# DeltaNet with routed experts: whole triangular inverses on VectorE, compact states, smaller tiles for Q times state and logits

## The chip, the cores and the metric

One core of one Trainium2 chip. The metric is the device time of one execution in microseconds (us), the median of several runs.

## The reference

Four batches, eight heads, 768 tokens, head dimension 48. A delta-rule attention runs token by token, and its output goes through a top-1 mixture of eight experts (3072 tokens, 384 -> 1024 -> 384):

```python
k_n = k / (norm(k) + 1e-06)
for t in range(S):
    y[:, :, t] = q_t @ state
    state = state + b_t * outer(k_t, v_t - k_t @ state)
x = y as (3072, 384)
logits = x @ w_gate; e = argmax; gate = softmax(logits)[e]
out = gate * (relu(x @ w1[e]) @ w2[e])
```

## The kernel before

**Blocks and steps.** The tokens are cut into 24 blocks of C = 32; a block holds all four batches (32 partitions each) and eight heads (four pairs p, and e = 0, 1 inside a pair). `step(c)` carries the state from block to block: K times state into `pc` (L366), R = V - K state on VectorE (L372), `pz` = inverse times R (L390), Z by ScalarE (L397), two half updates of `acc` in PSUM with copies of it into `states` behind each (L406, L417, L419), and the output `pq` = Q times state (L381) plus masked Q K times Z (L425). `states` holds 96 columns, two heads side by side with zeros between, so that Q times state uses all 128 rows at once.

**Scores.** `scores(c)` makes K K and Q K products of a block (L184); `keep_scores` masks them on VectorE into `gt` and `qk` (L203). In the loop, the block LEAD = 9 ahead of the step is scored; nine are scored ahead of the loop.

**Inverse.** Four blocks make a group g of 32 columns per partition (GS * H). `invert(g)`, a generator, transposes `gt` into `ut` (L222), takes norms by Newton steps, and inverts the two 16x16 triangles on the diagonal together: for each j a product (L281) and an addition (L286). `across(g, s)` fills the corner between them with two small products per block on PE (L316, L330), a ScalarE copy between and a VectorE addition behind (L335).

**Order.** The order is written out by hand. `fill(us)` advances the generators in `behind` until their rated costs (the numbers after `yield`) reach the amount; `chore(n)` runs n of the queued pieces of PE work. `chores` holds crossings, logits and ranks; `behind` holds inverses and routing. Engines run their own instructions in this order. One PSUM tile (`psA`) serves scores and crossings in turn; `psR` serves transposes, logits (L449) and ranks (L494, L497).

**Routing.** Batches of up to four blocks: logits, arg-max, ranks by a matmul with a triangular matrix, then a scatter of row numbers into `lists` by GpSimd (L533), one block each. The rows go to `xs` in DRAM.

**Experts.** Behind the attention, weights of experts 1 and 2 (L109, L110) take the memory that it used; then the lists are read, rows gathered, and eight experts computed in turn (L651 to L698). Expert 0's weights are loaded during step 12.

Of the kernel before, what the change touches and what calls it, by code (L numbers as in the profile page):

```python
# [13 lines left out]
FP32 = mybir.dt.float32  # L14
# [16 lines left out]
E = 8  # L31
# [9 lines left out]
LEAD = 9  # L41
# [4 lines left out]
def _f32_consts():  # L46

    p = np.arange(128)[:, None]
    j = np.arange(128)[None, :]
    rev = np.broadcast_to(E - np.arange(E), (128, E))
    base = np.broadcast_to(np.arange(E) * LIST, (128, E))
    more = np.arange(E)[:, None] * LIST + CAP + np.arange(MAXR)[None, :] * 128
    more = np.broadcast_to(more.reshape(1, -1), (128, E * MAXR))
    t, w = p % C, j[:, :C]
    own = t // (C // 2) == w // (C // 2)
    kk = 1.0 * (t == w) - ((t < w) & own) - (t // (C // 2) > w // (C // 2))
    return np.concatenate(  # L60
        [rev, base, more, p < j, np.ones((128, 128)), kk, t < w], axis=1
    ).astype(np.float32)
# [3 lines left out]
def kernel(  # L66
# [25 lines left out]
    def part(w):  # L92
# [4 lines left out]
    rev, base, further, upper, ones, mask_g, mask_q = (  # L97
        part(w) for w in (E, E, E * MAXR, 128, 128, C, C)
# [26 lines left out]
    psR = att.enter_context(tc.tile_pool(name="psR", bufs=1, space=PSUM))  # L125
# [5 lines left out]
    states = persist.tile([128, 2, 2 * NP, 2 * D], FP32, name="states")  # L131
# [4 lines left out]
    fdts = [persist.tile([128, GS * H, C], FP32, name=f"fdt{i}") for i in range(2)]  # L136

    kqs, kts, vts, qks, gts, ubs, norms, vss = {}, {}, {}, {}, {}, {}, {}, {}
    routed = []
    behind, chores = deque(), deque()  # L140

    def rows_of(b):
        return slice(C * b, C * b + C)

# [4 lines left out]
    def fill(us):  # L149
        while us > 0 and behind:  # L150
            cost = next(behind[0], None)
            if cost is None:
                behind.popleft()
            else:
                us -= cost
# [18 lines left out]
    def scores(c):  # L174
# [5 lines left out]
        for p in range(NP):  # L180
            for b in range(B):
                for e in range(2):
                    r = slice(64 * e, 64 * e + 64)
                    nc.tensor.matmul(  # L184
                        pa[rows_of(b), e, 64 * p : 64 * p + 64],
                        lhsT=kq[r, p, 0, rows_of(b)], rhs=kq[r, p, :, rows_of(b)],
# [4 lines left out]
    def keep_scores(c, pa):  # L191
# [7 lines left out]
        for out, part, mask in (  # L199
            (gts[g][:, H * s : H * s + H, :], view[:, :, :, 0:C], mask_g),  # L200
# [9 lines left out]
    def invert(g):  # L210


        gt = gts[g]
        W = C // 2
        ut = block.tile([128, C * C + C], FP32, name="ut")
        full = ut[:, 0 : C * C].rearrange("p (i j) -> p i j", j=C)
        diag = ut[:, 0 : C * C].rearrange("p (i j) -> p i j", j=C)
        ud = ut[:].rearrange("p (k n) -> p k n", k=2)[:, :, 0 : W * C].rearrange(
            "p k (i j) -> p k i j", j=C
        )  # L220
        ones_at = ut[:, 0 : C * C : C + 1]
        nc.vector.transpose(  # L222
            out=full.rearrange("p i j -> p j i"), in_=gt[:].rearrange("p s j -> p j s")
        )
        yield 1.15

        def short(name, bufs=None):
            return small.tile([128, C], FP32, name=name, **({"bufs": bufs} if bufs else {}))
# [3 lines left out]
        nc.vector.memset(full[:, W:C, 0:W], 0.0)  # L232
        yield 0.3
# [5 lines left out]
        yield 0.2  # L239
        r = seed[:].bitcast(FP32)  # L240
        for _ in range(3):
            t = short("nt", 3)
# [3 lines left out]
            yield 0.2  # L246
            nc.vector.tensor_tensor(out=t[:], in0=t[:], in1=r, op=OP.mult)
            yield 0.2
            rn = short("nr", 3)
# [3 lines left out]
            yield 0.2  # L253
# [3 lines left out]
        yield 0.2  # L257
        nc.vector.tensor_scalar(out=norm[:], in0=norm[:], scalar1=1e-6, scalar2=None, op0=OP.add)
        yield 0.2
        inv = short("inv")  # L260
        nc.vector.reciprocal(out=inv[:], in_=norm[:])
        yield 0.35
        norms[g] = small.tile([128, GS * H], FP32, name="normt", bufs=3)
        nc.vector.transpose(out=norms[g][:], in_=norm[:])
        wt = short("wt")
        nc.vector.tensor_tensor(out=wt[:], in0=inv[:], in1=inv[:], op=OP.mult)
        yield 0.3
        nc.vector.tensor_tensor(out=wt[:], in0=wt[:], in1=beta[:, g, :], op=OP.mult)
        yield 0.2
        w2 = wt[:].rearrange("p (k i) -> p k i", k=2)  # L270
        square = ud[:, :, :, 0:W]
        nc.vector.tensor_tensor(
            out=square, in0=square, in1=w2.unsqueeze(3).to_broadcast([128, 2, W, W]), op=OP.mult
        )
        nc.vector.memset(ones_at, 1.0)
        yield 0.75
        for j in range(W - 2, 0, -1):
            n = W - 1 - j
            tmp = block.tile([128, W * W // 2], FP32, name="tmp", bufs=3)
            tv = tmp[:, 0 : 2 * j * n].rearrange("p (k i w) -> p k i w", k=2, w=n)  # L280
            nc.vector.tensor_tensor(  # L281
                out=tv, in0=ud[:, :, 0:j, j].unsqueeze(3).to_broadcast([128, 2, j, n]),
                in1=ud[:, :, j, j + 1 : W].unsqueeze(2).to_broadcast([128, 2, j, n]), op=OP.mult,
            )
            yield 0.16 + 0.0021 * j * n
            nc.vector.tensor_tensor(  # L286
                out=ud[:, :, 0:j, j + 1 : W], in0=ud[:, :, 0:j, j + 1 : W], in1=tv, op=OP.add
            )
            yield 0.16 + 0.0021 * j * n
        nc.vector.tensor_tensor(  # L290
            out=square, in0=square, in1=w2.unsqueeze(2).to_broadcast([128, 2, W, W]), op=OP.mult
        )
        yield 0.7
        ub = block.tile([128, GS * H, C], FP32, name="ub", bufs=3)
        nc.vector.transpose(
            out=ub[:].rearrange("p s j -> p j s"), in_=full.rearrange("p i j -> p j i")
        )
        yield 1.15
        fdt = fdts[g % 2]
        nc.vector.transpose(  # L300
            out=fdt[:, :, 0:W].rearrange("p s i -> p i s"), in_=full[:, 0:W, :]
        )
        yield 0.6
        ubs[g] = ub
        for s in range(GS):
            chores.append(partial(across, g, s))

    def across(g, s):

        gt, ub, fdt = gts[g], ubs[g], fdts[g % 2]  # L310
# [43 lines left out]
    def step(c):  # L354
# [3 lines left out]
        pz = pc[:, :, 192:384].rearrange("q e (p w) -> q e p w", p=NP)  # L358
        if c == 0:
            R = vs  # L360
        else:
            for p in range(NP):
                for b in range(B):
                    for e in range(2):
                        r = slice(64 * e, 64 * e + 64)
                        nc.tensor.matmul(  # L366
                            pc[rows_of(b), e, D * p : D * p + D], lhsT=kq[r, p, 0, rows_of(b)],
                            rhs=states[r, b % 2, NP * (b // 2) + p, D * e : D * e + D],
                            start=(p == 0), stop=True, skip_group_check=True,
                        )  # L370
# [4 lines left out]
            )  # L375
        scale_v(c + 1)
        pq = psQ.tile([128, DM], FP32, name="pq")
        if c > 0:
            for p in range(NP):
                for b in range(B):  # L380
                    nc.tensor.matmul(  # L381
                        pq[rows_of(b), 96 * p : 96 * p + 96], lhsT=kq[:, p, 1, rows_of(b)],
                        rhs=states[:, b % 2, NP * (b // 2) + p, :],
                        start=(p == 0), stop=False, skip_group_check=True,
                    )
        chore()
        fill(1.2)
# [10 lines left out]
        keep_scores(c + LEAD, pa)  # L398

        def update(first):  # L400

            for p in range(NP):
                for b in range(B):
                    e = b // 2 if first else 1 - b // 2
                    at = D * (NP * (b // 2) + p)
                    nc.tensor.matmul(  # L406
                        acc[64 * e : 64 * e + D, b % 2, at : at + D],
                        lhsT=kt[rows_of(b), 2 * p + e, :], rhs=Z[rows_of(b), 2 * p + e, :],
# [378 lines left out]
```

## Time and profile before

| | before |
|---|---|
| median of three runs | 781.13 us (780.2 to 782.03) |
| profiled execution | 774.58 us, span 772.6 us |
| granted TensorE clock, mean | 0.78 |
| PE matmul busy | 609.1 us (79%), 12596 instructions |
| VectorE busy | 222.5 us (29%), 671 instructions |
| ScalarE busy | 142.6 us (18%), 407 instructions |
| GpSimd busy | 102.0 us (13%) |

PE is TensorE, DVE VectorE, ACT ScalarE, POOL GpSimd. The clock is the share of full speed that TensorE was granted. Busy times are unions over the span; each fp32 matmul appears as two pairs of weight load and matmul, a transpose as one. L numbers are lines of the kernel.

### The profile page before, as it was taken

The numbers are of one execution on the slowest core, as the hardware profiler recorded it, in microseconds if no ns is written. First come the engines' busy times: TensorE is split into PE (matmuls) and PEld (weight loads), VectorE is DVE, ScalarE is ACT, GpSimd is POOL, SyncE is SP. The second block draws the span as 40 slices with busy tenths as digits, with TensorE's granted clock in tenths as the row PEclk, the third lists the DMA queues.
The fourth block names the chain that finished last, engine by engine and source line by source line (L and its number), as shares of the span: only waits on it lengthen the run. The fifth ranks groups of instructions, "written<-read, shape, count | busy, mean of one in ns | idle before, by whom it ended". The sixth has DMA issues, their size and how long they took to land. (4 is left out here: it accounts for less than half of the span.)

```text
span 772.6 us, 27052 instructions
## 1 busy us (share of the span) xinstructions
PE 609.1 (79%) x12596; PEld 419.1 (54%) x12597; DVE 222.5 (29%) x671; ACT 142.6 (18%) x407; POOL 102.0 (13%) x107
## 2 busy tenths in 40 slices
PE   3268886777787578778782089999999999999992
PEld 2257775666676467666672045555555454545450
DVE  3963545155454524611221010101010101010100
ACT  0033221222322123222420000101010101010100
POOL 2000001100200100110103121313131313131010
PEclk9998555555576555555855579999999999999997
DMA  8402103220420620211102810124232423230000
GB/s 299 164 25 74 56 26 118 51 71 26 120 79 25 226 45 25 65 24 45 46 24 65 294 49 21 45 100 121 102 123 102 125 102 124 102 123 20 12 19 11
DMA packets 32339, 63.64 MB, mean 82 GB/s; under 512 B 5942, under 2 KB 23782, under 8 KB 32224
## 3 DMA queue, kind: packets, MB, share of 16 engines
q1 hardware_dynamic: 26640, 51.94, 21.0%
q0 software_dynamic: 4608, 9.47, 4.1%
q8 instruction: 99, 1.62, 0.9%
q10 hardware_dynamic: 976, 0.48, 0.3%
q14 instruction: 16, 0.13, 0.1%
HBM read 53.10 MB, written 10.35 MB: 82 GB/s over the span
## 5 line engine op out<-in xcount | busy, mean ns | idle before, releaser
L660 PE MATMUL phe<-xTe,w1t 128*128 128x448 f32 x384 | 147.6, 545 | 0.0
L676 PE MATMUL pye<-w2t,hT 128*128 128x384 f32 x384 | 125.1, 486 | 0.0
L660 PEld LDWEIGHTS phe<-xTe,w1t 128*128 128x128 f32 x384 | 72.9, 192 | 69.5 <-issue 67.2
L676 PEld LDWEIGHTS pye<-w2t,hT 128*128 128x128 f32 x384 | 73.0, 190 | 51.6 <-issue 3.0
L533 POOL DMA_INDIRECT lists<-ids,ri x24 | 23.5, 978 | 385.9 <-DVE ut L286 142.1
L665 DVE TENSOR_SCALAR hT<-phe 128x448 f32<-128x448 f32 x32 | 20.0, 624 | 126.7 <-PE phe L660 126.7
L640 POOL DMA_INDIRECT out_dram<-y,rows x24 | 24.0, 999 | 210.9 <-ACT y L685 177.5
L406 PE MATMUL acc<-Z,kt 32*48 32x48 f32 x1472 | 41.0, 265 | 13.0 <-issue 6.6
L419 DVE COPY states<-acc 48x384 f32<-48x384 f32 x46 | 25.8, 560 | 88.6 <-ACT states L417 88.5
L184 PE MATMUL pa<-kq 64*32 64x64 f32 x1536 | 29.2, 303 | 27.8 <-issue 18.9
L349 ACT ACTIVATE vs<-vt,normt 128x48 f32<-128x48 f32 x192 | 45.5, 322 | 0.0
L669 ACT ACTIVATE hT<-phe 128x448 f32<-128x448 f32 x32 | 17.4, 543 | 151.6 <-PE phe L660 151.6
L651 PE MATMUL px<-ident,xin 128*128 128x128 f32 (+1 forms) x96 | 18.9, 304 | 32.7 <-issue 30.6
L406 PEld LDWEIGHTS acc<-Z,kt 32*48 32x48 f32 x1472 | 32.6, 170 | 21.0 <-issue 10.4
L425 PE MATMUL pq<-Z,qk 32*32 32x48 f32 x1536 | 34.4, 260 | 9.0 <-issue 8.2
L390 PE MATMUL pc<-R,ub 32*32 32x48 f32 x1472 | 32.5, 260 | 10.6 <-DVE R L372 7.5
L184 PEld LDWEIGHTS pa<-kq 64*32 64x32 f32 x1536 | 22.8, 145 | 31.7 <-issue 20.7
L655 DVE COPY xTe<-px 128x448 f32<-128x448 f32 x24 | 14.1, 612 | 88.6 <-PE px L651 88.6
L316 PE MATMUL po<-ub,gt 32*32 32x16 f32 x1536 | 25.8, 206 | 17.2 <-issue 8.8
L417 ACT ACTIVATE states<-acc 48x384 f32<-48x384 f32 x46 | 22.2, 483 | 88.2 <-PE acc L406 88.2
L330 PE MATMUL po<-m,fdt 32*32 32x16 f32 x1536 | 26.5, 205 | 13.5 <-issue 7.5
L449 PEld LDWEIGHTS pr<-wg,xT 128*128 128x128 f32 x144 | 30.1, 304 | 11.6 <-ACT xT L443 6.9
(96 smaller groups left out, 628.2 us busy)
## 6 DMA issues: line engine op xcount, KB each, us to landing
kq<-in_kq_t_dram SPq DMA_DIRECT2D x24, 512.0 KB, 5.5
w1t<-in_moe_w_dram SPq DMA_DIRECT2D x8, 1536.0 KB, 6.4
w2t<-in_moe_w_dram SPq DMA_DIRECT2D x8, 1536.0 KB, 7.1
kt<-in_k_tok_dram SPq DMA_DIRECT2D x24, 192.0 KB, 3.7
vt<-in_v_tok_dram SPq DMA_DIRECT2D x24, 192.0 KB, 4.0
xs<-xg SPq DMA_DIRECT2D x5, 770.0 KB, 5.0
xs<-xg SPq DMA_DIRECT2D x1, 577.5 KB, 3.8
lists<-ids,ri POOLq DMA_INDIRECT x24, 3.8
```

What stands on the lines that cost most here:

```text
L184: nc.tensor.matmul(pa[rows_of(b), e, 64 * p : 64 * p + 64], lhsT=kq[r, p, 0, rows_of(b)], rhs=kq[r, p, :, rows_of(b)], start=True, stop=Tr ...
L316: nc.tensor.matmul(po[rows_of(b), 0, W * h : W * h + W], lhsT=gt[rows_of(b), sh, :], rhs=ub[rows_of(b), sh, W:C], start=True, stop=True, s ...
L330: nc.tensor.matmul(po[rows_of(b), 0, W * h : W * h + W], lhsT=fdt[rows_of(b), sh, :], rhs=m1[rows_of(b), h, :], start=True, stop=True, ski ...
L349: nc.scalar.activation(out=vss[c][:, h, :], in_=vt[:, h, :], func=AF.Copy, scale=norms[g][:, H * s + h : H * s + h + 1],)
L390: nc.tensor.matmul(pz[rows_of(b), h % 2, h // 2, :], lhsT=ub[rows_of(b), H * s + h, :], rhs=R[rows_of(b), h, :], start=(c == 0 and h < 2), ...
L406: nc.tensor.matmul(acc[64 * e : 64 * e + D, b % 2, at : at + D], lhsT=kt[rows_of(b), 2 * p + e, :], rhs=Z[rows_of(b), 2 * p + e, :], start ...
L419: nc.vector.tensor_copy(out=out, in_=src)
L425: nc.tensor.matmul(pq[rows_of(b), D * h : D * h + D], lhsT=qk[rows_of(b), h, :], rhs=Z[rows_of(b), h, :], start=(c == 0 and h == 0), stop= ...
L449: nc.tensor.matmul(pr[:, DM + E * i : DM + E * i + E], lhsT=xT[:, s, :], rhs=wg[:, s, :], start=(s == 0), stop=(s == NK - 1), skip_group_c ...
L640: nc.gpsimd.indirect_dma_start(out=out, out_offset=bass.IndirectOffsetOnAxis(ap=index, axis=0), in_=y[0:w, :], in_offset=None, bounds_chec ...
L660: nc.tensor.matmul(ph[:], lhsT=w1t[:, s, f * 128 : f * 128 + 128], rhs=xT[:, s, :], start=(s == 0), stop=(s == NK - 1),)
L676: nc.tensor.matmul(py[:], lhsT=hT[:, f, t * 128 : t * 128 + w], rhs=w2t[:, f, :], start=(f == 0), stop=(f == NF - 1),)
```

## The change

The inverse of a group is made whole, 32x32, on VectorE for all groups but the first (K = 1; group 0 keeps K = 2 and the crossing). `ut` is laid out the other way round; its transposes are cut in four pieces each. Rated costs are changed, and `fill` takes turns between the first two generators in `behind`, with a queue `soon` for routing ahead of them. `mask_g` is a full triangle, `mask_0` the old one.

`states` is compact, 48 columns; K and Q blocks are loaded without padding rows, in two transfers of 48 partitions. Q times state uses the same 64-row tiles as K times state. Odd heads' tokens of batch b stand in the partitions of batch b ^ 1 (`rows_at`); V, K and beta are laid out so on the host. The copies of `acc` into `states` are two on ScalarE behind the second update; a small read `seen` stands between the updates. Logits are made in four 32-column parts. Transposes, logits and ranks use the one `psA` tile; `psR` is gone. Eight blocks are scored ahead of the loop (FRONT), then one or two a step until all 24 are scored in step 10. Before each fourth step the inverse of its group is drained.

```diff
-LEAD = 9
+FRONT = 8
+LEAD = 13
...
     def fill(us):
-        while us > 0 and behind:
-            cost = next(behind[0], None)
+        while us > 0 and (soon or behind):
+            from_ = soon or behind
+            cost = next(from_[0], None)
...
+            us -= cost
+            if from_ is behind and len(behind) > 1:
+                behind[0], behind[1] = behind[1], behind[0]
...
-            nc.sync.dma_start(out=kqs[c][:], in_=kq_t[c])
+            for e in range(2):
+                nc.sync.dma_start(out=kqs[c][head(e)], in_=kq_t[c, e])
...
         gt = gts[g]
-        W = C // 2
+        K = 1 if g else 2
+        W = C // K
...
+        for j in range(0, C, 8):
+            nc.vector.transpose(
+                out=full[:, j : j + 8, :], in_=gt[:, :, j : j + 8].rearrange("p s j -> p j s")
+            )
+            yield 0.3
...
+        parts = [(0, W, W)] if K > 1 else [(0, W // 2, W // 2), (W // 2, W, W)]
...
         for j in range(W - 2, 0, -1):
             n = W - 1 - j
...
-            yield 0.16 + 0.0021 * j * n
+            yield 0.09 + 0.00105 * K * j * n
...
+        def by_state(out, i, at):
+            for p in range(NP):
+                for b in range(B):
+                    for e in range(2):
+                        nc.tensor.matmul(
+                            out[at(b, e), e, D * p : D * p + D],
+                            lhsT=kq[head(e), p, i, rows_of(b)],
+                            rhs=states[head(e), b % 2, NP * (b // 2) + p, :],
+                            start=(p == 0), stop=(i == 0), skip_group_check=True,
+                        )
...
+        if turned:
+            logits(*turned.pop())
+        pq = psQ.tile([128, 2, 512], FP32, name="pq")
+        if c > 0:
+            by_state(pq, 1, lambda b, e: rows_of(b))
+        chore()
         scale_v(c + 1)
...
-        fill(1.2)
+        fill(2.6)
...
-        pa = scores(c + LEAD)
+        more = []
+        while scored[0] < min(NS, c + LEAD + 1, FRONT + 1 + c + (c + 1) // 2):
+            for old in more:
+                keep_scores(*old)
+            more = [(scored[0], scores(scored[0]))]
+            scored[0] += 1
...
         if c < NS - 1:
-            update(True)
-        for h in range(H):
+            update(0)
+            seen = small.tile([128, 2], FP32, name="seen")
+            nc.scalar.activation(
+                out=seen[0 : 64 + D], in_=acc[0 : 64 + D, :, 0], func=AF.Copy
+            )
+        for p in range(NP):
+            for b in range(B):
+                for e in range(2):
+                    nc.tensor.matmul(
+                        pq[rows_of(b), e, D * p : D * p + D], lhsT=qk[rows_at(b, e), 2 * p + e, :],
+                        rhs=Z[rows_at(b, e), 2 * p + e, :],
...
+        if c < NS - 1:
+            update(1)
+            for k in range(2):
+                nc.scalar.activation(
+                    out=states[0 : 64 + D, k].rearrange("q s w -> q (s w)"),
+                    in_=acc[0 : 64 + D, k, 0:DM], func=AF.Copy,
+                )
...
+        for s in range(NK):
             for b in range(B):
                 nc.tensor.matmul(
...
+                    pt[rows_of(b), 1, 0:E], lhsT=xT[:, s, rows_of(b)], rhs=wg[:, s, :],
                     start=(s == 0), stop=(s == NK - 1), skip_group_check=True,
                 )
+        nc.scalar.activation(out=lgs[ss[0]][:, c - ss[0], :], in_=pt[:, 1, 0:E], func=AF.Copy)
...
+    for c in range(FRONT):
+        keep_scores(c, scores(c))
+        if c in (GS - 1, GS):
+            fill(4.0)
+        if c == GS + 1:
+            while not ubs:
+                fill(0.1)
+            chore(2)
...
     for c in range(NS):
         load_kq(c + LEAD + 2)
         load_tok(c + 3)
+        if c % GS == 0:
+            while c // GS not in ubs:
+                fill(0.1)
+        step(c)
         chore(2)
+        turn(c)
+        fill(2.0)
+        soon.extend(ranked)
+        ranked.clear()
+        fill(1.8)
```

## Rows read from the trace of the kernel before

**Rows 1.** Busy time by stretches (us, instructions), granted clock, DMA share, GB/s.
```profile
228.00:404.00 176.00, 133.05 (x5115) 113.80 (x5115) 63.53 (x213) 51.07 (x162) 11.67 (x12) 0.59 0.21 58
445.00:772.00 327.00, 310.83 (x992) 165.39 (x990) 42.24 (x72) 35.48 (x64) 68.68 (x68) 0.97 0.23 77
```
**Rows 2.** Timeline of PE in step 17: start, duration, work, count, idle before.
```profile
321.17 1.03 PE L366 MATMUL pc<-states,kq 64*32 64x48 f32 x64
322.13 1.50 PE L381 MATMUL pq<-states,kq 128*32 128x96 f32 x32
323.56 1.45 PE L449 MATMUL pr<-wg,xT 128*128 128x8 f32 x6
325.62 1.50 PE L390 MATMUL pc<-R,ub 32*32 32x48 f32 x64 [0.60 <-DVE R L372]
327.73 0.89 PE L406 MATMUL acc<-Z,kt 32*48 32x48 f32 x32 [0.61 <-ACT Z L397]
328.55 0.86 PE L425 MATMUL pq<-Z,qk 32*32 32x48 f32 x32
...
330.42 0.89 PE L406 MATMUL acc<-Z,kt 32*48 32x48 f32 x32
331.24 1.05 PE L316 MATMUL po<-ub,gt 32*32 32x16 f32 x64
333.64 1.18 PE L330 MATMUL po<-m,fdt 32*32 32x16 f32 x64 [1.36 <-issue]
334.76 0.90 PE L439 MATMUL pr<-ident,xg 128*128 128x128 f32 x3
335.59 0.69 PE L366 MATMUL pc<-states,kq 64*32 64x48 f32 x35
```
**Rows 3.** Timeline: starts of L390 in steps 0, 4, 11 and 23.
```profile
45.65 1.48 PE L390 MATMUL pc<-vs,ub 32*32 32x48 f32 x64
...
108.64 0.88 PE L390 MATMUL pc<-R,ub 32*32 32x48 f32 x64 [0.79 <-DVE R L372]
...
227.96 0.88 PE L390 MATMUL pc<-R,ub 32*32 32x48 f32 x64 [0.25 <-DVE R L372]
...
404.51 1.50 PE L390 MATMUL pc<-R,ub 32*32 32x48 f32 x64
```
**Rows 4.** Timeline of ScalarE: eight V scalings, a copy of states.
```profile
224.78 1.90 ACT L349 ACTIVATE vs<-vt,normt 128x48 f32<-128x48 f32 x8
...
231.62 0.48 ACT L417 ACTIVATE states<-acc 48x384 f32<-48x384 f32 x1 [2.22 <-PE acc L406]
```
**Rows 5.** VectorE groups by line and shape: count, busy us, mean ns, idle before.
```profile
L295 DVE STREAM_TRANSPOSE ub<-ut 128x1024 f32<-128x1024 f32 x6 | 12.2, 2040 | 0.2
...
L290 DVE TENSOR_TENSOR ut<-ut,wt 128x512 f32<-128x512 f32 x6 | 4.2, 692 | 0.2
...
L286 DVE TENSOR_TENSOR ut<-ut,tmp 128x112 f32<-128x112 f32 x12 | 3.3, 274 | 0.4
```
**Rows 6.** Timeline of VectorE: two independent products, then two dependent ones.
```profile
217.13 0.43 DVE L203 TENSOR_TENSOR gt<-pa,cf 128x256 f32<-128x256 f32 x1 [5.59 <-PE pa L184]
217.47 0.41 DVE L203 TENSOR_TENSOR qk<-pa,cf 128x256 f32<-128x256 f32 x1
...
224.38 0.19 DVE L243 SCALAR_TENSOR_TENSOR nt<-ss,seed 128x32 f32<-128x32 f32 x1
224.61 0.19 DVE L247 TENSOR_TENSOR nt<-nt,seed 128x32 f32<-128x32 f32 x1
```
**Rows 7.** Timeline of PE in step 13: the hole in L425.
```profile
269.55 0.70 PE L425 MATMUL pq<-Z,qk 32*32 32x48 f32 x24 [4.34 <-issue]
```
**Rows 8.** Timeline of VectorE: the last transpose of group 0.
```profile
33.76 1.05 DVE L300 STREAM_TRANSPOSE fdt<-ut 128x512 f32<-128x512 f32 x1
```
**Rows 9.** Timeline: last scatter of row numbers, first weight load behind it.
```profile
416.53 0.97 POOL L533 DMA_INDIRECT lists<-ids,ri  x1 [2.95 <-DMA lists<-ids,ri]
...
420.11 0.38 SPq L109 DMA_DIRECT2D w1t<-in_moe_w_dram  x1
```

More of the change, by code (lines that the diff above doesn't have):

```diff
@@ L95, in part @@
         return a
-    rev, base, further, upper, ones, mask_g, mask_q = (
-        part(w) for w in (E, E, E * MAXR, 128, 128, C, C)
+    rev, base, further, upper, ones, mask_g, mask_0, mask_q = (
+        part(w) for w in (E, E, E * MAXR, 128, 128, C, C, C)
     )
@@ L252, in invert @@
             )
-            yield 0.2
+            yield 0.12
             r = rn[:]
@@ L293, in invert @@
-        yield 0.7
-        ub = block.tile([128, GS * H, C], FP32, name="ub", bufs=3)
[L295 to L303, printed above, removed]
+            yield 0.09 + 0.00105 * K * j * n
+        yield from scaled(False)
+        ub = block.tile([128, GS * H, C], FP32, name="ub", bufs=3)
@@ L361, in step @@
         else:
[L362 to L370, printed above, removed]
+            by_state(pc, 0, rows_at)
             R = work.tile([128, H, D], FP32, name="R")
@@ new lines, in step @@
+        for p in range(NP):
[4 more added lines that the diff above has]
+                        rhs=Z[rows_at(b, e), 2 * p + e, :],
+                        start=(c == 0 and p == 0), stop=True, skip_group_check=True,
+                    )
+        ss = first[c]
+        if c == ss[0]:
+            xgs[c] = work.tile([128, GS, ROW], FP32, name="xg")
+            lgs[c] = small.tile([128, GS, E], FP32, name="lg")
@@ new lines, in turn @@
+    def turn(c):
+        ss = first[c]
+        pt = psA.tile([128, 2, 512], FP32, name="pt", tag="pa")
+        for s in range(NK):
+            nc.tensor.transpose(
+                pt[:, 0, 128 * s : 128 * s + 128],
+                xgs[ss[0]][:, c - ss[0], s * 128 : s * 128 + 128], ident[:],
+            )
+        if counted:
+            counted.pop()(pt)
+        xT = work.tile([128, NK, 128], FP32, name="xT")
+        nc.scalar.activation(
+            out=xT[:].rearrange("p s w -> p (s w)"), in_=pt[:, 0, 0:DM], func=AF.Copy
+        )
+        turned.append((c, xT, pt))
@@ L424, in step, with logits @@
+    def logits(c, xT, pt):
+        ss = first[c]
+        for s in range(NK):
             for b in range(B):
                 nc.tensor.matmul(
-                    pq[rows_of(b), D * h : D * h + D], lhsT=qk[rows_of(b), h, :],
-                    rhs=Z[rows_of(b), h, :],
-                    start=(c == 0 and h == 0), stop=True, skip_group_check=True,
-                )
-        fill(0.4)
-        if c < NS - 1:
-            update(False)
-        return pq
-    def logits(xg, i, pr):
-        for s in range(NK):
-            nc.tensor.transpose(
-                pr[:, 128 * s : 128 * s + 128], xg[:, i, s * 128 : s * 128 + 128], ident[:]
-            )
-        xT = work.tile([128, NK, 128], FP32, name="xT")
-        nc.scalar.activation(
-            out=xT[:].rearrange("p s w -> p (s w)"), in_=pr[:, 0:DM], func=AF.Copy
-        )
-        def second():
-            for s in range(NK):
-                nc.tensor.matmul(
-                    pr[:, DM + E * i : DM + E * i + E], lhsT=xT[:, s, :], rhs=wg[:, s, :],
+                    pt[rows_of(b), 1, 0:E], lhsT=xT[:, s, rows_of(b)], rhs=wg[:, s, :],
```

285 lines of the change are left out of this document (132 added, 153 removed).

## The prediction

> **What bounds the kernel now.** I read the table by stretches first [rows 1]. The expert stage (445 to the end) has TensorE (PE) busy for 310.8 of 327 us at a granted clock of 0.97; nothing in the change touches it. [...] The timeline of one step on PE alone [rows 2] shows how a step is spent: 14.42 us from one K times state (L366) to the next, nearly all of it in program order on PE. The first triangular crossing (L316), its copy and the second (L330) take from 331.24 to 334.76, 3.5 us with a 1.36 us "issue" hole in them; Q times state (L381) 1.43, logits (L449) 1.45, Q K times Z (L425) 1.87 to the start of the second update. The rest is the recurrence: L366, R, L390, Z, two updates (L406). So the change must be read as PE time removed per step, and then one must ask whether DVE, which takes over the crossings' work, still fits under what is left.
>
> The steps' marks are the starts of L390, R's product with the inverse [rows 3]: step 0 at 45.65, step 4 at 108.64, step 11 at 227.96, step 23 at 404.51. I forecast these four again, then the tail.
>
> **A late step, no scores (11 to 22).** PE in the new order, at the low clock, start to start from [rows 2]: K times state 0.96; logits; Q times state, now 64 pairs of the shape of L366, 0.96 for 1.43; L390 with the wait for Z 2.11 (325.62 to 327.73); update 0.82; Q K times Z; update 0.82; states. Three terms have no row. Logits become 24 pairs of 128 rows by 32 columns with 8 moving columns. From below: L316's spacing, 64 pairs in 1.05, gives 0.4; from above, not faster than today's 1.45. [...] Q K times Z now alternates between eight tiles of the array, not four: between L366's 0.96, which also has eight, and the 1.43 that four tiles cost in L390; I take 0.96. The states are now two ScalarE copies one after the other; one takes 0.48 [rows 4], so with a start gap of 0.4 and hand-overs of 0.15 each side 1.2, of which the transposes (0.83) cover their own time; DVE's copies go, and with them the wait of the second update, but a small read ("seen") stands there instead, hidden under the 64 pairs of Q K times Z. R (0.55 by interpolation between the 256-element mask product and the 512-element product, [rows 5, 6]) is hidden under logits and Q times state. Sum 8.3. Code loading is extra: a PE idle that ends on "issue" comes back at block boundaries of the instruction stream, and a long one is 4.34 us [rows 7], in the step after the one that asks for expert 0's weights. In this step it shows 1.36 in one piece; I take 1.1 a step, as the step without crossings has 18% fewer pairs of weight load and matmul (347 for 425, by the counts there [rows 2]). A late step is 9.4. From the other side: 14.42 less the crossings 3.5, logits 1.0 and the R wait 0.6, 0.5 for Q times state and 0.7 for Q K times Z is 8.1, plus 0.4 of states that the crossing no longer hides, and a stall of 0.9 that moves elsewhere: 9.4.
>
> **What VectorE must do in it.** Durations by shape [rows 5]: a product of 112 elements 274 ns, of 512 elements 692 ns, so 0.157 + 0.00104 per element; a 1024-element transpose 2.04. A whole 32x32 inverse needs 60 loop instructions on 9920 elements (today 28 on 2240), four scalings (1.1 us a pair), some 22 short ones and eight transposes of 256 elements (about 0.6 each, from 2.04/4 and a fixed part). In busy time that is 19.7 + 2.2 + 4 + 4.5 = 30 us a group; today some 18. But what counts is start to start. The timeline has two independent products that start 0.34 apart though one takes 0.43, and two dependent ones that start 0.23 apart though one takes 0.19 [rows 6]. So an instruction costs its duration less 0.085 beside an independent one, plus 0.035 behind its own input. Two groups in turn: 23 us a group (30 less 0.085 for each of some 90 instructions); one alone: 33. [...]
>
> The order written out gives each step costs of 6.4 (2.6 behind R, 3.8 at its end), and a group is rated 22.5 there, near its 23 interleaved. So DVE needs 0.55 + 6.6 = 7.2 in a late step, under 9.4: hidden. In steps 4 to 10 the mask products add 0.8 a scored token block.
>
> **Steps 4 to 10.** There are ten blocks scored in seven steps. A step with one block: 8.3 less the 0.6 wait for Z, which the scores now cover, plus 1.2 for them (64 pairs of 64 columns, between L366's 1.03 and L390's 1.50 [rows 2]), plus 1.1 of code loading beside K/Q loads: 10.0. With two blocks the second must wait for DVE to read the first out of the one PSUM tile, queued behind 2.6 us of inverse: another 1.2 + 1.0, 12.2. Four and three of them: 76.6. Two batches' routing each stall DVE about 1.5, since the sum over exp waits for ScalarE behind eight V scalings of 1.90 together [rows 4]: 3. Before step 8 the inverse of group 2 is rated some 1.8 short, and draining it in turns costs 3.6. Sum 83.
>
> **Steps 0 to 3.** Here DVE paces. Group 1 must be whole before step 4 and runs alone until block 11 is scored: of its 33 alone some 30 us remain, with 7 for group 2's share, 2 for R, 5 for six blocks' masks, 7 where it stands behind PE for the three crossings of group 0, and some 7 of waits for scores: 58, against 63 now.
>
> **Start.** Group 0 is inverted as today: L300 ends at 34.8 and L390 starts 10.85 later [rows 3, 8]. The crossing now comes ahead of scores 6 and 7, and there are eight blocks, not nine, so the inverse is done one mask pair (0.8) sooner: 34.0, two crossing products with copy and addition 3, scores and masks of two blocks 2 times 2.05, and the next crossing's product with its wait 1.5, together 42.6, three earlier.
>
> **Tail.** The next stage's weights (L109) are issued when the last scatter of row numbers has landed [rows 9], 15.6 after L390 of step 23. The scatters go one at a time: the last waited 2.95 us for the one before it. Now three of batch 5 are issued some 4.5 us later behind that L390, with logits, routing and ranks each one step on, so the fourth lands at about 20.8: 5 us lost. The other DMAs don't matter: 15 K/Q blocks are loaded ahead, in two transfers each of 3/4 of the bytes; one weight load during step 12 keeps its price, 4.
>
> **The sum**, in the profiled execution: 42.6; step 4 at 42.6 + 58 = 101; step 11 at 101 + 83 = 184; step 23 at 184 + 12 times 9.4 + 4 + 3 (draining before step 12) = 304; weights issued at 325 instead of 420.1; and 352.5 from there to the end, unchanged: 677 for 772.6. The execution takes 2.0 more than its span (774.6), and the median of the runs shown, 781.1, is 6.5 above it; 677 + 2 + 6.5 = 686.
>
> **Rivals.** A, VectorE becomes the bound: each of its instructions costs what a dependent one does. For: 60 short instructions a group, in program order ahead of R. Against: 0.34 for 0.43 [rows 6]. Then 6.4 of rated work takes 9.4 (33 for 22.5), a step of 4 to 17 goes to 11.3, 1.3 more on average, and the drains double: 18 + 10, 714. [...] B, the granted clock rises to its upper level as PE's holes go: at that level L390 takes 0.88 for 1.50 [rows 3]. Then a late step is 7.4 and a middle one, held by DVE, a little under 10: 12 times 2.0 + 5, 657. Against: the mean is 0.59 where PE is already busy for 76% [rows 1]. C, code loading takes the gain back: 2.2 a step and not 1.1 in 19 steps with blocks fetched as often per us, 21, and 5 more beside the weight load: 712. D, slower than before: scores, crossings, transposes, logits and ranks now share one PSUM tile, and each hand-over waits for a reader on DVE or ScalarE. If PE stood at it for more than 95/19 = 5.0 us a step beyond the sum, that is behind the whole 3.8 of rated inverse and a second wait, the kernel would be at 783 and above. Against: the order puts the readers ahead of the long fills, the second block's masks excepted. That Q K times Z gains nothing from eight tiles would cost 0.5 times 24, 12 us, and logits at their upper bound 24: inside the range.
>
> **How the numbers follow.** The forecast (670 to 702) 0.56, A 0.18, C 0.12, B 0.11, D 0.03. The range 650 to 735 takes in A, B and C, and, beyond A and C, the bounds of the logits or of the eight tiles for part of the way. A measurement of this kernel can tell about 0.2%; faster by more than that 0.96, within 0.01, slower 0.03.
>
> **What would show it.** Right: L316 and L330 only for group 0; late steps of 9 to 10 us; DVE idle before R in them; starts of two groups' loop instructions closer than one's duration; clock 0.55 to 0.7. A shows as PE waiting for R in most steps; B as L390 of 0.88 throughout; C as "issue" idle of over 40 us; D as PE waiting for masks or lg. I would be most wrong if logits and R don't hide each other, or if the order of DVE's queue blocks R.

## The result and the profile after

The changed kernel took 718.4 us (median) where the kernel before took 781.6 beside it: ratio 0.919 with a 95% interval of 0.913 to 0.924; a second measurement gave 0.919 again (0.915 to 0.924). That is faster, by 63 us where 95 were forecast: inside the range of 650 to 735, well above the forecast of 686. The profiled execution took 713.3, its span is 711.4.

From the page of the changed kernel, first the span, the busy times (share of the span, instructions) and the instruction queue (packets, MB):
```profile
span 711.4 us, 24428 instructions
PE 549.3 (77%) x11204; PEld 359.3 (51%) x11205; DVE 235.4 (33%) x802; ACT 144.1 (20%) x434; POOL 99.9 (14%) x105
q8 instruction: 88, 1.44, 0.9%
```
and the same queue on the page of the kernel before:
```profile
q8 instruction: 99, 1.62, 0.9%
```
TensorE lost 1392 matmuls (12596 before) and as many weight loads, VectorE gained 131 instructions. The queue that brings instructions fell from 99 packets to 88; 1.44 MB in 88 packets is 16.4 KB each, and the 22409 matmuls and weight loads make 255 for each packet.

The four marks, on the timeline of PE: the starts of R's product with the inverse (now L414) in steps 0, 4, 11 and 23; compare [rows 3]:
```profile
43.17 0.82 PE L414 MATMUL pc<-vs,ub 32*32 32x48 f32 x26
...
106.39 0.78 PE L414 MATMUL pc<-R,ub 32*32 32x48 f32 x27
...
203.57 0.70 PE L414 MATMUL pc<-R,ub 32*32 32x48 f32 x24
...
337.17 0.79 PE L414 MATMUL pc<-R,ub 32*32 32x48 f32 x29 [1.25 <-DVE xg L540]
```

| stretch | before | forecast | after |
|---|---|---|---|
| start to step 0 | 45.7 | 42.6 | 43.2 |
| steps 0 to 3 | 63.0 | 58 | 63.2 |
| steps 4 to 10 | 119.3 | 83 | 97.2 |
| steps 11 to 22 | 176.6 | 120 | 133.6 |
| step 23 to the weights' issue | 15.6 | 21 | 22.3 |
| from there to the end | 352.5 | 352.5 | 352.0 |

The two ends came as forecast, the steps between did not. One late step on PE, which answers to [rows 2] (start, duration, work, count, idle before):
```profile
284.60 1.50 PE L414 MATMUL pc<-R,ub 32*32 32x48 f32 x64
286.71 0.89 PE L435 MATMUL acc<-Z,kt 32*48 32x48 f32 x32 [0.61 <-ACT Z L426]
287.53 1.02 PE L451 MATMUL pq<-Z,qk 32*32 32x48 f32 x64
288.48 0.89 PE L435 MATMUL acc<-Z,kt 32*48 32x48 f32 x32
289.30 0.90 PE L479 MATMUL pt<-ident,xg 128*128 128x128 f32 x3
290.13 1.06 PE L388 MATMUL pc<-states,kq 48*32 48x48 f32 x64
291.12 0.38 PE L496 MATMUL pt<-wg,xT 128*32 128x8 f32 x24
291.42 0.69 PE L388 MATMUL pq<-states,kq 48*32 48x48 f32 x50
294.23 0.41 PE L388 MATMUL pq<-states,kq 48*32 48x48 f32 x14 [2.12 <-issue]
294.57 1.50 PE L414 MATMUL pc<-R,ub 32*32 32x48 f32 x64
```
The terms of the sum are there at or below their forecast sizes (Q K Z 0.95, logits 0.30, L414 with the wait for Z 2.11; of the 1.2 for the states only the transposes' 0.83 is left), and without the hole the step takes 7.9 us where the sum said 8.3. The hole is 2.12 us and ends on "issue". This is one of the shorter steps: the twelve late ones take 11.1 us on average. What PE waited for between steps 0 and 23, before (total, times, longest), without its "issue" rows:
```profile
PE pr L439 <- DVE rk L525: 9.7, 5, 2.4
...
PE pc L390 <- DVE R L372: 7.5, 9, 1.3
...
PE po L330 <- ACT m L321: 5.3, 13, 0.5
PE acc L406 <- ACT Z L397: 5.0, 8, 0.8
PE po L316 <- DVE ub L335: 4.1, 6, 1.3
PE pr L449 <- ACT xT L443: 3.6, 6, 0.7
```
and after:
```profile
PE pq L388 <- issue: 17.0, 15, 2.4
PE acc L435 <- issue: 12.6, 12, 1.9
PE pc L414 <- issue: 8.8, 11, 1.9
PE acc L435 <- ACT Z L426: 7.8, 12, 1.2
PE pc L414 <- DVE R L400: 6.0, 5, 2.7
PE pa L197 <- PE pa L197: 5.8, 5, 2.1
PE pa L197 <- issue: 5.7, 6, 1.4
```
Waits for other engines shrank, but "issue" idle grew, from 43.6 us in 46 holes to 50.7 in 54, although there is less to issue.

### The profile page after: what moved, and what is told of

It is laid out like the page before. It is cut to its first block, busy times and chain, and to the rows that moved or that the text cites. A ratio compares the mean times of both kernels' runs of the same rounds, so it can differ in the third digit from the quotient of the medians.

```text
span 711.4 us, 24428 instructions
## 1 busy us (share of the span) xinstructions
PE 549.3 (77%) x11204; PEld 359.3 (51%) x11205; DVE 235.4 (33%) x802; ACT 144.1 (20%) x434; POOL 99.9 (14%) x105
## 3 DMA queue, kind: packets, MB, share of 16 engines
q8 instruction: 88, 1.44, 0.9%
## 5 line engine op out<-in xcount | busy, mean ns | idle before, releaser
L704 PEld LDWEIGHTS phe<-xTe,w1t 128*128 128x128 f32 x384 | 72.9, 192 | 69.9 <-issue 68.0
L435 PE MATMUL acc<-Z,kt 32*48 32x48 f32 x1472 | 45.3, 279 | 21.2 <-issue 12.6
L197 PE MATMUL pa<-kq 48*32 48x64 f32 x1536 | 32.6, 310 | 29.8 <-issue 13.1
L306 DVE TENSOR_TENSOR tmp<-ut 128x220 f32<-128x220 f32 (+14 forms) x164 | 50.6, 317 | 2.3
L311 DVE TENSOR_TENSOR ut<-ut,tmp 128x220 f32<-128x220 f32 (+14 forms) x164 | 50.6, 318 | 2.2
L414 PE MATMUL pc<-R,ub 32*32 32x48 f32 x1472 | 38.1, 276 | 14.1 <-issue 6.9
L388 PE MATMUL pq<-states,kq 48*32 48x48 f32 x1472 | 29.4, 274 | 17.2 <-issue 17.0
L197 PEld LDWEIGHTS pa<-kq 48*32 48x32 f32 x1536 | 24.3, 148 | 36.1 <-issue 15.7
L414 PEld LDWEIGHTS pc<-R,ub 32*32 32x32 f32 x1472 | 32.3, 159 | 18.7 <-issue 9.6
L729 ACT ACTIVATE y<-pye,xin 128x384 f32<-128x384 f32 x16 | 9.3, 580 | 133.2 <-PE pye L720 133.2
L695 PEld LDWEIGHTS px<-ident,xin 128*128 128x128 f32 (+1 forms) x96 | 11.2, 148 | 48.7 <-issue 44.0
```

The costliest lines, as they stand in the source:

```text
L197: nc.tensor.matmul(pa[rows_at(b, e), e, 64 * p : 64 * p + 64], lhsT=kq[head(e), p, 0, rows_of(b)], rhs=kq[head(e), p, :, rows_of(b)], star ...
L306: nc.vector.tensor_tensor(out=tv, in0=ud[:, :, j + 1 : W, j].unsqueeze(3).to_broadcast([128, K, n, j]), in1=ud[:, :, j, 0:j].unsqueeze(2). ...
L311: nc.vector.tensor_tensor(out=ud[:, :, j + 1 : W, 0:j], in0=ud[:, :, j + 1 : W, 0:j], in1=tv, op=OP.add)
L388: nc.tensor.matmul(out[at(b, e), e, D * p : D * p + D], lhsT=kq[head(e), p, i, rows_of(b)], rhs=states[head(e), b % 2, NP * (b // 2) + p, ...
L414: nc.tensor.matmul(pz[rows_of(b), h % 2, h // 2, :], lhsT=ub[rows_of(b), H * s + h, :], rhs=R[rows_of(b), h, :], start=(c == 0 and h < 2), ...
L435: nc.tensor.matmul(acc[head(e), b % 2, at : at + D], lhsT=kt[rows_at(b, e), 2 * p + e, :], rhs=Z[rows_at(b, e), 2 * p + e, :], start=(c == ...
```

## The experiments

**Supply theory:** TensorE's instructions arrive in blocks of 256 at a pace of about 4 us, and the loop cannot go faster than its blocks. **Execution theory:** the loop is paced by what TensorE executes, so columns and tile shapes count. **VectorE theory:** the inverses pace it. The table has, from step 0 to step 23, the time and the matmuls and weight loads in that stretch over 256, from the table by stretches of each profile; the ratio is to the kernel before on the same chip. Ratios come from several executions, times between the marks from the one that was profiled.

| kernel | us | blocks | us a block | ratio [95%] |
|---|---|---|---|---|
| before | 358.9 | 83.7 | 4.29 | 1 |
| changed | 294.0 | 73.1 | 4.02 | 0.919 [0.913, 0.924] |
| changed, again | 292.5 | 73.1 | 4.00 | 0.919 [0.915, 0.924] |
| 1 wide columns | 293.3 | 73.1 | 4.01 | 0.921 [0.913, 0.930] |
| 2 more instructions | 337.4 | 84.6 | 3.99 | 0.980 [0.969, 0.992] |
| 3 no turns | 294.3 | 73.1 | 4.02 | 0.928 [0.926, 0.931] |
| 4 crossings back | 368.8 | 93.1 | 3.96 | 1.032 [1.027, 1.037] |
| 5 logits whole | 287.2 | 69.9 | 4.11 | 0.920 [0.911, 0.929] |
| 6 Q wide, with a sum | 286.3 | 67.4 | 4.25 | 0.911 [0.902, 0.921] |
| 7 odd pairs | 276.3 | 67.4 | 4.10 | 0.904 [0.900, 0.908] |
| 8 odd pairs, logits whole | 285.8 | 64.1 | 4.46 | 0.906 [0.903, 0.909] |
| 9 odd pairs, first group whole | 270.7 | 64.8 | 4.18 | 0.897 [0.895, 0.900] |
| 10 odd pairs, split copy | 313.7 | 67.4 | 4.65 | 0.943 [0.939, 0.948] |
| 11 as 9, Q behind Z | 274.7 | 64.5 | 4.26 | 0.900 [0.895, 0.905] |

**1. Columns without instructions.**
```diff
-    pq[..., D * p : D * p + D], ... rhs=states[..., at0, :]
+    pq[..., 2 * D * p : 2 * D * p + 2 * D], ... rhs=states[..., at0 and the slot behind it]
```


> The changed kernel, but each Q times state matmul streams 96 columns instead of 48 (the second half is never read; the output is the same). TensorE gets exactly the same number of instructions and more to execute. Supply theory (the loop is paced by the delivery of TensorE's instructions, one block of 256 in about 4.0 us: 73 blocks between 43 and 337 us, 51 us of idle time put down to issue): no change against the changed kernel's 718, at most +5 us, the added work falls into the idle stretches at block ends. Execution theory (the loop is paced by what TensorE executes): 64 pairs at 48 columns took 1.03 us, 32 pairs of 96 columns in the kernel before 1.4, so +0.4 to +1.8 us a step, 23 steps, +9 to +40 us.


Measured: 0.921 against 0.919, and the loop took 293.3 us. Twice the columns of a sixth of the loop's matmuls cost nothing that can be seen, and execution theory, which wanted 9 us or more, falls here by the marks; the ratio's interval alone would still allow 9. PE was busy for 227.7 us instead of 218.4 and idle on "issue" for 45.4 instead of 50.7: the longer matmuls went into the holes.

**2. Instructions without columns.**
```diff
+    for p, b, e: nc.tensor.matmul(pq[..., 192 + 8 * p : 200 + 8 * p], lhsT=kq[..., 1, ...],
+                                  rhs=states[..., 0:8], start=False, stop=True, ...)
```


> The changed kernel with 32 further matmuls of only 8 columns after Q times state in each of 23 steps, into columns of PSUM that nobody reads. The trace shows each such matmul as two pairs of weight load and matmul, so these are 128 instructions a step, half a block. Supply theory: 0.5 x 23 blocks x 4.0 us = +46 us against 718, about 764. Execution theory: 64 pairs in at most the 1.03 us that 64 pairs of 48 columns took, 24 pairs of 8 columns took 0.45 us, so +1.0 us a step, +23 us, less where it lies in idle time.


Measured: a ratio of 0.980, 47 us more than the changed kernel by that run's kernel before (774.2 times 0.061); between the marks 43.4. Half a block a step at 4.0 us was forecast at 46. The trace shows the blocks themselves. Timeline of PE from one "issue" hole to the third:
```profile
277.96 0.48 PE L388 MATMUL pq<-states,kq 48*32 48x48 f32 x23 [0.39 <-issue]
278.17 0.22 PE L412 MATMUL pq<-states,kq 48*32 48x8 f32 x2
278.22 0.30 PE L388 MATMUL pq<-states,kq 48*32 48x48 f32 x4
278.24 0.21 PE L412 MATMUL pq<-states,kq 48*32 48x8 f32 x3
278.24 0.28 PE L388 MATMUL pq<-states,kq 48*32 48x48 f32 x1
278.31 0.84 PE L412 MATMUL pq<-states,kq 48*32 48x8 f32 x59
279.07 1.01 PE L423 MATMUL pc<-R,ub 32*32 32x48 f32 x36
281.72 0.85 PE L423 MATMUL pc<-R,ub 32*32 32x48 f32 x28 [1.64 <-issue]
283.15 0.89 PE L444 MATMUL acc<-Z,kt 32*48 32x48 f32 x32 [0.58 <-ACT Z L435]
283.97 1.02 PE L460 MATMUL pq<-Z,qk 32*32 32x48 f32 x64
284.92 0.40 PE L444 MATMUL acc<-Z,kt 32*48 32x48 f32 x4
285.56 0.88 PE L444 MATMUL acc<-Z,kt 32*48 32x48 f32 x28 [0.25 <-issue]
```
From hole to hole 23+2+4+3+1+59+36 = 128 matmuls, then 28+32+64+4 = 128: with a weight load each, 256 instructions, 3.76 and 3.84 us apart. The holes fall where a block ends, in the middle of a product as well as between two, not where anything is waited for. With the semaphore instructions of TensorE's queue counted too (49 in this loop), 67 of 67 "issue" holes stand at the same place modulo 256, within two instructions. In the kernel before 45 of 46 do, in the changed kernel 42 of 54; the other twelve there are shorter than 0.5 us. The packets agree: 85 of the instruction queue in this loop, where the matmuls and weight loads make 84.6 blocks. A block takes these 3.8 us here, and between 3.45 and 6.2 us over all neighbouring holes of this loop.

**3. The two groups not interleaved.**
```diff
-    if from_ is behind and len(behind) > 1:
-        behind[0], behind[1] = behind[1], behind[0]
```


> The changed kernel without the two lines that swap the two groups after each VectorE instruction, so one group's inverse is issued to its end before the next begins. Supply theory (TensorE's instruction delivery paces the loop): VectorE has slack, the same 73 blocks are delivered, 0 to +8 us against the changed kernel, most of it in steps 0 to 4 where the first groups are awaited. VectorE theory: each operation waits for the one before it, about 0.1 us more for each of some 60 operations of each of 5 groups, and the late groups delay their steps: +10 to +30 us.


Measured: 294.3 us between the marks, as the changed kernel; VectorE was busy there for 183.3 us and not 164.0. The ratio is 0.9% higher than the changed kernel's, some 7 us, of which the profiled span shows 2.5 to 3.3; where the rest lies I can't say. VectorE theory, which wanted 10 us or more, falls for the loop: interleaving saves VectorE time that nobody waits for there.

**4. The whole inverses undone.**
```diff
-    K = 1 if g else 2
+    K = 2
```
(the first mask for every group, three fdt tiles, and the crossings of each step issued behind the step before)


> The changed kernel with the whole inverses undone: every group, not only the first, is inverted as two 16x16 blocks on VectorE and completed by 64 matmuls a step on TensorE, which are 256 instructions of TensorE, one whole block, in each of 20 steps more. Supply theory: 20 x 4.0 us = +80 us, which is more than the whole gain of the change (63 us), so about 798 on a chip where the kernel before takes 781. Execution theory: the two passes took 1.65 and 1.6 us a step in the kernel before, 20 x 3.25 = +65 us, less what lies in idle stretches, +30 to +65 us. VectorE theory: fewer elements on VectorE, so no change or faster, -10 to +10 us.


Measured: 1.032, or 87 us above the changed kernel (0.113 of 772); 74.8 between the marks for 20 blocks. The inverses alone are worth more than the whole change gained. The pace is the fastest of all, 3.96.

**5. Logits whole.**
```diff
-    for b in range(B): nc.tensor.matmul(pt[rows_of(b), 1, 0:E], lhsT=xT[:, s, rows_of(b)], ...)
+    nc.tensor.matmul(pt[:, 1, 0:E], lhsT=xT[:, s, :], ...)
```


> The changed kernel with the logits as in the kernel before, three 128x128 matmuls a step instead of twelve 128x32: 6 pairs in the trace instead of 24, 36 instructions a step fewer, more to execute (1.45 us for 6 pairs in the kernel before against 0.45 us for 24). Supply theory: 24 x 36 / 256 = 3.4 blocks x 4.0 us = -13 us against 718, about 705. Execution theory: +1.0 us x 24 = +24 us, about 742.


Measured: the same ratio, and 6.8 us less between the marks of one profile. Both were wrong: three blocks fewer give part of their 13 us at most, and the slower matmuls do not cost 24. The smaller logits tiles of the change bought 1.0 us a step of execution with 36 instructions, and were worth nothing that can be told within the interval of some 7 us either way.

**6. Q times state in 96 columns, with a sum on VectorE.**
```diff
-    for e in range(2): nc.tensor.matmul(out[at(b, e), e, ...], lhsT=kq[head(e), p, i, ...], rhs=states[head(e), ...])
+    nc.tensor.matmul(pq[rows_of(b), p % 2, at : at + 96], lhsT=kq[:, p, 1, ...], rhs=states[:, b % 2, ...])
+    nc.vector.tensor_tensor(out=half, in0=half, in1=pq[:, :, 192:384]..., op=OP.add)
```
(here and in 7 to 11, K and Q are also loaded with padding rows in one transfer a block again)


> The changed kernel with Q times state undone: states in 96 columns with zeros beside them, 16 matmuls of 128x32 tiles with 96 columns instead of 32 of 48x32 with 48, in columns of their own, and their sum with Q K Z formed by one more VectorE operation a step. 64 instructions a step fewer; the two copies of the states on ScalarE move 768 columns each instead of 384, about +0.4 us each on the way to the next step; the added sum stands ahead of the transposes. Supply theory: 23 x 64 / 256 = 5.75 blocks x 4.0 us = -23 us, less what the longer copies and the sum put on the path (up to 0.8 us x 23 = 18 us): -23 to -5 us against 718. Execution theory: 32 pairs of 96 columns took 1.4 us against 1.03 us for 64 of 48, +0.4 us, and the copies +0.8 us: +9 to +28 us.


Measured: 0.911, some 6 us faster than the changed kernel by ratio, 7.7 between the marks; the intervals of the two ratios overlap, so this run alone does not show a gain. Execution theory wanted slower by 9 us or more. "Issue" idle fell to 36.9 us, but PE now stood 13.9 us for R and 7.2 for the sum.

**7. The same without the sum.**
```diff
-    def rows_at(b, e): return rows_of(b ^ e)
+    def rows_at(b, p): return rows_of(b ^ (p & 1))
```
(the states' banks, the odd tokens of the inputs and beta follow, Q times state as in 6, accumulating)


> The changed kernel with Q times state in 16 matmuls of 96 columns again, but without the sum on VectorE that the run with wide states needed: the tokens of odd pairs of heads, not of odd heads, are put into neighbouring partitions, so that both heads of a pair share one bank and Q K Z can be added on top of Q times state in PSUM. 64 instructions a step fewer than in the changed kernel, the copies of the states 768 columns each. Supply theory: the run with the sum lost 8 us of transposes waiting for the sum and 8 us more waiting for R; without these -15 to -23 us against the changed kernel (ratio to the kernel before 0.89 to 0.90). Execution theory: as in the run with the sum, at best +9 us.


Measured: 0.904, 11 to 12 us faster than the changed kernel by ratio, 17.7 between the marks, below what supply theory wanted by ratio and inside it by marks. (The profiled execution took 692.6 us, where the median of the four is 696.6.) So Q times state in small tiles, one part of the change, cost time by itself. "Issue" idle is 33.8 us, and a wait that blocks had hidden comes up; PE's waits in the loop of this kernel:
```profile
PE pc L387 <- ACT states L477: 11.5, 31, 0.6
PE acc L444 <- ACT Z L435: 7.4, 12, 0.8
```

**8. With whole logits too** (the diffs of 5 and 7).


> The same with the logits in three whole 128x128 matmuls too, 100 instructions a step fewer than in the changed kernel. Supply theory: 23 x 100 / 256 = 9 blocks x 4.0 us = -36 us at most; with the run of whole logits alone, which gained some 2 to 7 us, -20 to -30 us (ratio 0.88 to 0.895). Execution theory: +9 us for Q times state and +24 us for the logits.


Measured: 0.906, as without, at 4.46 us a block. (Between the marks it is 9.5 us above 7, but the execution profiled here lies 3.2 us above its median and that of 7 lies 3.9 below.) Supply theory missed by 8 to 20 us. "Issue" idle is down to 23.5 us, so at 64 blocks most of the time is something else; that it is the path through execution and hand-overs is argued from this, not shown.

**9. The first group whole** (on 7; K = 1 for every group).


> The run with odd pairs in neighbouring partitions and Q times state in 96 columns (ratio 0.904), and the first group's inverse whole on VectorE as well: no crossing on TensorE is left, 4 x 256 instructions, four blocks, less in steps 0 to 3, or just before step 0. Supply theory: -4 x 3.9 = -16 us between step 0 and step 4, whose 63 us are 17 blocks of 3.9 us, against a later step 0, since the first inverse has some 18 us of multiplications and additions instead of 6 on VectorE with nobody to interleave with, +10 us or more: the marks 0 to 4 shrink by 12 to 16 us and the whole by 0 to 6 us. Theory that the start steps wait for VectorE (the two groups ahead of time): step 0 later by 10 us or more and no shorter steps 0 to 4, +10 us.


Measured: 0.897, 694.8 us beside 712.8 for the changed kernel on the same chip, 2.5% below it, the fastest of all. Step 0 begins at 49.6 instead of 41.8, steps 0 to 3 take 51.5 instead of 62.3. Of the four blocks, 2.5 come out of these steps (12.8 for 15.3), the rest from ahead of step 0, and the 10.8 us gained are a little less than the 12 to 16 that supply theory wanted. VectorE is busy in these steps as long as before, 40.6 us for 39.7, so those steps, which I had called VectorE's, were not paced by it. The kernel beside it:


> The changed kernel itself once more, as the measure for the two runs beside it on the same chip: ratio to the kernel before 0.919 as at first (0.913 to 0.924).


It was 0.919. Tables by stretches (PE busy, weight loads, VectorE, ScalarE, GpSimd, granted clock, DMA share, GB/s), of the changed kernel first, then of the same kernel again:
```profile
43.20:337.20 294.00, 218.42 (x9364) 177.70 (x9357) 164.00 (x620) 103.41 (x354) 19.85 (x20) 0.59 0.23 65
43.80:336.30 292.50, 215.53 (x9361) 177.42 (x9354) 163.88 (x620) 103.42 (x354) 19.88 (x20) 1.00 0.23 65
```
The column of the granted clock reads 0.59 and 1.00, but this is no test of the clock. R's product on the timeline of the second profile:
```profile
282.50 1.50 PE L414 MATMUL pc<-R,ub 32*32 32x48 f32 x64
```
It takes 1.50 us here, as it does at a granted clock of 0.50 in the late step shown above, while the kernel before has 0.88 for the same 64 pairs at 1.00 (step 4 in [rows 3]; the clock records of that trace have 1.00 from 107.6 to 111.0 us). In none of the 24 steps of either profile does it take less than 1.50. The trace of the second profile has no record of the clock before 392.6 us, so its 1.00 for the loop is no reading of the level. No run here has the loop at the upper level throughout, and none shows what the clock is worth to it.

**10. One states copy on VectorE** (on 7).
```diff
+    if e == 0: nc.scalar.activation(out=out, in_=src, func=AF.Copy)
+    else: nc.vector.tensor_copy(out=out, in_=src)
```


> The run with odd pairs in neighbouring partitions (ratio 0.904), with one of the two 768-column copies of the states on VectorE instead of both on ScalarE, as the kernel before had it. In that run K times state waited 11.5 us in 31 places for ScalarE's copies. If the block supply alone paces, the wait is only filled by the next hole and nothing changes (0 to -3 us); if the path from the update to the next step counts between the holes, up to -11 us, unless VectorE's copy stands behind operations of the inverse in its order.


Measured: 30 us slower than 7 (0.039 of 774). Waits of PE between 45 and 335 us, then VectorE's timeline:
```profile
PE pc L423 <- DVE R L409: 35.7, 16, 5.1
PE pc L387 <- DVE states L482: 10.1, 17, 0.7
```
```profile
131.67 0.96 DVE L482 COPY states<-acc 48x768 f32<-48x768 f32 x1 [3.14 <-ACT states L480]
132.66 0.41 DVE L310 TENSOR_TENSOR ut<-ut,tmp 128x234 f32<-128x234 f32 x1
```
VectorE stands 3.14 us before the copy with the inverse's instructions queued behind it; it then catches up in front of R, and PE waits for that. The warning in the expectation came true. It suggests that moving such a copy to ScalarE was a gain of the change on its own; with the changed kernel's shorter copies of 384 columns that was not tried.

**11. Q times state behind Z, narrow states for K** (on 9).


> The run with odd pairs in neighbouring partitions and the first group whole (ratio 0.897), with Q times state moved behind Z, where it covers ScalarE's copy of Z, and with narrow states (two copies of 384 columns) for K times state beside the wide ones, which are copied later, behind the transposed rows. TensorE's instructions are the same in number. In the run before, K times state waited 11.3 us for the copies and the update 7.2 us for Z. If only the block supply counts, nothing is gained, 0 to -3 us; if the path between the holes counts too, -5 to -18 us; if ScalarE, which gets 0.87 us a step more, becomes late with the scaled V, up to +20 us.


Measured: 0.900, no gain. The waits for the copies fell to 1.3 us and those for Z to nothing; "issue" idle rose from 35.1 to 37.7 us and that for R from 1.7 to 15.9. Waits taken off the path came back as others.

## Why the forecast was right in direction and 32 us off in size

**What failed is one term above all:** code loading, put at 1.1 us a late step because the step has 18% fewer pairs than one that showed a hole of 1.36. Measured: 50.7 us of "issue" idle in 23 steps, 2.2 a step, which is rival C's figure; its price, 712, is 6 below the measured 718.4. (C's sign, over 40 us of "issue" idle, would not have told by itself, as the kernel before already had 43.6.) The idle is uneven. Steps 4 to 10 have 19.2 us of it, 2.7 a step, and that is 11.5 of the 14.2 us by which they ran over. Steps 11 to 22 have 19.8, or 1.65 a step, which is 6.6 above the 13.2 forecast, of 13.6 over. The 4 us beside expert 0's weights and the 3 for draining, also in that stretch of the forecast, do not show as such: its longest hole is 2.3 us. So more than the 6.6 came in from elsewhere, and it does not stand as idle time in the rows; part of it lies under the modelled ends of the matmuls in front of the holes, which last 0.28 us although the next starts 0.015 later where there is no hole (64 pairs in 0.96), and it was not broken down further.

The reasoning treated a hole as a cost of each block. The runs show a pace: when the work inside a block gets shorter than the block's delivery, the difference becomes a hole. Before, 358.9 less 43.6 us of holes over 83.7 blocks left 3.77 us of other work and waits a block, near the delivery; after, 294.0 less 50.7 over 73.1 left 3.33. The forecast sped up the work and kept the holes small. By the count, with the 4.0 us that the runs gave afterwards, it would have been: a late step of 347 pairs is 2.7 blocks, 10.8 us, where the steps took 11.1 and I wrote 9.4. That the measured time still lay in the range of 650 to 735 is owed to the rivals that were priced into it, not to the forecast's own sum.

**Where the 64.9 us between the marks came from:** 10.6 blocks at 4.02 are 43; the other 22 are waits for other engines that the new order took away. Experiment 2 holds this up: with the blocks of the kernel before (84.6 for 83.7) in the new order, it needs 337.4 us, 21.5 less than that kernel. The largest of those waits in the rows above, transposes behind rk (9.7), logits behind xT (3.6) and the crossing's copy (5.3), are gone or below 1 us. Of the blocks, the inverses took 20 away, and Q times state in small tiles gave 5.75 back and the logits 3.4. (Experiments 4 and 7 measure the first two at 75 and 18 us between the marks, the 18 from an execution 3.9 us below its median.)

**Steps 0 to 3** were put down to VectorE, 58; they took 63.2 for 16.3 blocks, 3.9 us each, with 2.7 us of waiting for R, and experiment 9 shortened them by taking 2.5 blocks out while VectorE's busy time in them stayed the same. That step named the wrong engine.

**What held.** Terms with a near row: Q K Z on eight tiles (0.96, measured 0.95), K and Q times state (0.96, and 0.99 for K in the step shown, where Q has the hole), Z with its wait 2.11. The low clock of the sum is 0.50 in the step of [rows 2], by the table by stretches. No run shows the 0.45 that the sum takes for the logits; their 24 pairs took 0.30 to 0.44 from start to start. The states' copies took less of PE's time than 1.2 a step, since the transposes cover most of them. The start (42.6, 43.2) and the tail, whose loss of 5 us came as 6.7. Timeline of the last scatter and the first weight load; compare [rows 9]:
```profile
356.19 0.97 POOL L578 DMA_INDIRECT lists<-ids,ri  x1 [2.57 <-DMA lists<-ids,ri]
...
359.44 0.38 SPq L111 DMA_DIRECT2D w1t<-in_moe_w_dram  x1
```
VectorE's interleaving held too, and more than held. Its timeline in the changed kernel, two groups in turn:
```profile
148.10 0.42 DVE L311 TENSOR_TENSOR ut<-ut,tmp 128x150 f32<-128x150 f32 x2
148.45 0.42 DVE L306 TENSOR_TENSOR tmp<-ut 128x130 f32<-128x130 f32 x2
148.79 0.42 DVE L311 TENSOR_TENSOR ut<-ut,tmp 128x130 f32<-128x130 f32 x2
```
Two operations in each 0.35 us, where one of 130 elements lasts 0.29 (by [rows 5], and in the mean of this trace).

**The rivals.** A (VectorE bound): PE waited 6.0 us for R in all, and experiment 3 shows interleaving not to matter to the loop; wrong. Nor does each instruction cost what a dependent one does: the rows above have two starts in 0.35 us at 0.29 each, where the dependent ones of [rows 6] start 0.23 apart at 0.19. B (clock): it did not come about. Its sign was 0.88 us for R's product throughout, and that took 1.50 or more in every step; what the upper level would have been worth was not tested. C was right in kind, and near in size. D (shared PSUM tile): the rows that can be such waits, scores behind scores, make 5.8 us in all; wrong.

**What the trace adds on the blocks, and what stays open.** It has each packet of the instruction queue q8 with its times. In the loop of experiment 2 there are 85 of them, 16384 bytes each, which took 1.08 us in the median and 0.88 to 3.34, and no two start less than 3.33 us apart. In the median of the 67 holes, TensorE goes on 1.40 us after a packet has ended, and the next packet starts 1.15 us after that. One behind the other, these make 3.6 us, an estimate from the three medians, and a longer packet goes with a longer block: in the changed kernel's loop the next one starts 3.61 us (median) behind the start of a packet that took under 1.0 us, and 4.09 behind one that took over 1.3. How busy the DMA engines were with other data while a packet was under way did not go with the time that it took (correlation -0.13). No run without the loads of data was made, and none varied the parts of this chain.

## What to carry to other kernels

Where a loop is made of tiny matmuls, count TensorE's instructions, divide by 256, and compare time per block with what other stretches show before summing durations: below about 4 us a block here, shorter work mostly made longer "issue" holes. A split into smaller tiles that runs faster can lose by its own instruction count, and moving work to an engine with slack pays by the instructions it takes off the queue of the one that is short of them. Once blocks are no longer short (here at some 65 to 67), the next hand-over takes the place of the last, so each further saving should be measured by itself.

## What the runs showed of the hardware that I had not expected

In this loop TensorE's instructions came at about 4 us for each 256: 3.96 to 4.02 us in six profiles from 73 to 93 blocks, with packets never less than 3.31 us apart in the changed kernel and 3.33 in experiment 2. Doubling the columns of 64 matmul records a step cost nothing that was seen; adding 128 instructions a step cost 43 us over 23 steps. And a granted clock of 1.00 in a table by stretches has to be read beside the durations of the matmuls: in one profile it stood for a loop whose matmuls took 1.50 us, as at 0.50, because the trace had no record of the clock there.
